# Blocks 2 and 3 of a fused recurrence and max-out kernel: second layer by seven products, the last product over three banks, and three chunks' transposes in halves

## The chip, the cores and the metric

The kernel runs on one core of a Trainium2 chip. The metric is the device time of one execution in microseconds (us), as the median of several runs. A core has five engines with instruction streams of their own: TensorE (PE in the profile, with its weight loads as PEld), VectorE (DVE), ScalarE (ACT), GpSimd (POOL) and SyncE (SP), which here only issues DMAs. An engine runs its stream in program order and waits on semaphores for the others.

## The reference

Two stages, one after the other. A gated recurrence runs over 6144 time steps, for 4 sequences of 256 features. Its 24576 x 256 output goes through a layer that takes the larger of two products and multiplies it with a third matrix.

```python
def _attn_ref(x, f_logit, lower_bound):          # x, f_logit: (4, 6144, 256)
    sig = 1.0 / (1.0 + np.exp(-f_logit))
    f = lower_bound[None, None, :] + (1.0 - lower_bound[None, None, :]) * sig
    i = 1.0 - f
    for t in range(S):
        h = f[:, t] * h + i[:, t] * x[:, t]
        y[:, t] = h
    return y

def _moe_ref(x, w1, w2, w_out):                  # (24576, 256), (256, 1024) twice, (1024, 256)
    h1 = x @ w1
    h2 = x @ w2
    g = np.maximum(h1, h2)
    return g @ w_out
```

## The kernel before

**Tiling.** Time is cut into 48 blocks of 512 steps, 12 to a sequence. Features lie on the 128 partitions in two halves, so a block's y is two tiles of 128 x 512. Blocks 0 to 3 come in chunks of their own; from chunk 4 on a chunk holds 1024 steps, that is a pair of blocks. Pair p is blocks 2p and 2p + 1, and belongs to chunk p + 2. Pairs from `PAIR0` = 2 on are worked on as pairs.

**Input.** GpSimd loads f_logit and x of a chunk with a cast to 16 bits into a scratch in DRAM (`fetch`, L96). `cross(c)` (L143) issues two transposing DMAs from SP, scratch to the tiles `fT` and `xT` (L148), then a tiny GpSimd copy of one element of fT (`pool_waits`, L341), behind which the loads of chunk c + 1 are issued. So each chunk's load follows the landing of the fT before it.

**Recurrence.** A gate is a sigmoid on ScalarE (`gate` L197 for blocks 1 to 3, `pair_gate` L273 for a quarter of a pair: one half of the features, one block). On VectorE follow two `decay` instructions (L207), one `drive` (L217) and two scans (L224) per block. The scan writes y into the same tile that later holds the block's hidden values.

**First layer** (`first_layer`, L428). max(h1, h2) is written as h1 + ReLU(h2 - h1), with the difference of the weights in `wd`. One slot is one of 8 groups of 128 hidden units: two matmuls of 128 x 512 into half of a `dT` tile. Two dT tiles of two banks each exist. Each second slot ends with a ReLU on ScalarE (L442), which empties a dT tile.

**Second layer.** It multiplies the 8 hidden groups by w_out, and the two halves of y by the product w1 w_out (`w13`): ten left factors of 128 rows, for each of 4 groups of 128 tokens. Done directly (`second_layer`, L462, blocks 0 to 3) that is 40 matmuls with 256 columns, called in eight pieces of five. A copy then leaves each of two banks, on ScalarE for blocks 0 and 3 and on VectorE for 1 and 2 (L489).

For the pairs it is done with seven products instead of eight of half the width (`sevenths`, L517): the two blocks, the two halves of the inner sum and the two halves `lo` and `hi` of the columns are a 2 x 2 by 2 x 2 product. VectorE makes four sums of hidden tiles (`sum1` to `sum4`, L499; sum3 first, sum2 from sum3, sum4 from sum2). The right factors' sums t1 to t4 are made once. Each product is 20 steps, a step being one matmul of 128 columns, so that a pair is 140 steps (`NSEV`), over three banks X, E and B:

- X takes block 2p's first inner half; `seed` then copies X into bank B with ScalarE (L543).
- E takes sum1 (steps 20 to 39); a `snapshot` to SBUF follows (L549).
- X goes on with sum2 (from step 40), a snapshot follows; B takes its second product and is copied out (L559); X takes sum3 and leaves with an add of a snapshot (L561).
- E takes sum4 and leaves with an add; X takes the last product (from step 120) and is copied out.

For the last pair of all (`end`) the last product is split: groups 0 and 1 go on in bank X, groups 2 and 3 each go into a fresh bank Y (one of the dT tiles) and get the snapshot of X added on leaving (L582). Each leaves with a store of its own, on the queues of SP and ScalarE.

**Order.** The order is written out by hand. Blocks 2 and 3 run their first layer with one piece of direct second layer of the block before behind each slot (L747 to L768). From pair 2 on, a loop over 16 slots per pair issues a slot of first layer, then steps of the sevens of the pair before, as many as `due` has grown by, then a `cross` at slot 2, then gates of the next pair at slots 4, 6, 12 and 14, then from `seq` what VectorE has to do, each entry with a key in units of ninths of a slot. During pair 2 the second layer of block 3 runs directly in seven of the slots, and its last piece in pair 3.

## Time and profile before

| | us |
|---|---|
| median of 7 runs | 378.54 |
| lowest, highest | 377.94, 380.01 |
| the profiled execution | 378.82 |
| its span, first to last instruction | 377.0 |
| TensorE at its clock | granted 1.000 of full speed |

Some groups from the page, by line, with their count and mean duration:

| line | what | count | mean ns |
|---|---|---|---|
| L434 | first layer, matmul of 512 columns | 768 | 379 |
| L480 | direct second layer, matmul of 256 columns | 160 | 273 |
| L643 | step of the sevens, matmul of 128 columns | 3080 | 219 |
| L442 | ReLU out of dT, ScalarE | 192 | 1023 |
| L499 | sum of hidden tiles, VectorE | 88 | about 1480 |
| L561 | leave with an add, VectorE | 44 | 683 |
| L549 | snapshot, ScalarE | 44 | 587 |
| L148 | transposing DMA, fT | 22 | 5.8 us to landing |
| L148 | transposing DMA, xT | 22 | 5.0 us to landing |

Matmuls are pipelined: the next begins before the one before has ended, so their durations add up to more than the time. What one costs is seen from start to start, in the chain that ended last. The same holds, less strongly, for VectorE and ScalarE.

Three stages can be told apart: the start to 11 us with weights and first blocks, a start-up with direct second layers to 56 us, and then 20 pairs alike. At the end, from 363 us on, only the last pair's sevens and its stores are left.

### The profile page before, as it was taken

To read this page: it belongs to the slowest core of one execution; us is meant where nothing else is said; L and a number is where in the kernel's file an instruction comes from. 1 tells how busy PE (TensorE), PEld (TensorE's weight loads), DVE (VectorE), ACT (ScalarE), POOL (GpSimd) and SP (SyncE) were. 2 spreads that over 40 slices of the span, in tenths; PEclk is the share of its full clock that TensorE was granted. 3 is DMA by queue.
4 is the path that set the end of the run, shared out by engine and by line. 5 is a ranking of instruction groups with operands and counts; after the bars stand their busy time and mean duration, and the time that the engine had idled before them with its cause. 6 is when DMAs were issued, how large, how long until landed. Compare 5 with 4: busy or idle time off the path is not lost.

```text
span 377.0 us, 9634 instructions
## 1 busy us (share of the span) xinstructions
PE 367.8 (98%) x4156; PEld 280.1 (74%) x4156; DVE 338.1 (90%) x408; ACT 303.2 (80%) x412; POOL 38.5 (10%) x80
## 2 busy tenths in 40 slices
PE   6899999999999999999999999999999999999995
PEld 5577767777777777777777777777777777777784
DVE  5796889999999999999999999999999999999762
ACT  4866798888888798788888888887988888888752
POOL 1401111110110100210101101101101101000000
PEclk9999999999999999999999999999999999999999
DMA  8999989999999979999989969999999989940223
GB/s 267 233 202 247 223 171 197 206 202 220 279 187 192 295 122 243 266 164 219 273 156 254 275 135 200 284 184 225 263 187 265 249 148 235 196 184 2 114 113 112
DMA packets 104543, 77.17 MB, mean 205 GB/s; under 512 B 93298, under 2 KB 95348, under 8 KB 103796
## 3 DMA queue, kind: packets, MB, share of 16 engines
q1 hardware_dynamic: 101536, 51.19, 60.2%
q0 software_dynamic: 2544, 25.17, 34.7%
q8 instruction: 32, 0.52, 0.6%
q10 hardware_dynamic: 420, 0.20, 0.2%
q14 instruction: 11, 0.09, 0.1%
HBM read 53.48 MB, written 48.23 MB: 270 GB/s over the span
## 4 chain that ended last, share of the span: by engine, by line
PE 95%; DMA 2%; ACT 1%; SPq 0%; DVE 0%; issue 0%; DVEq 0%
PE ps L643 45%; PE dT L434 44%; PE ps L480 5%; DMA r<-in_moe_w_dram 2%; PE ps L174 1%; PE ps L390 0%; SPq L117 0%; ACT r L345 0%; ACT S L349 0%; PE ps L376 0%; DVE osb L561 0%; DVE osb L582 0%; ACT sn L574 0%; PE dT L643 0%; DVEq L561 0%
## 5 line engine op out<-in xcount | busy, mean ns | idle before, releaser
L442 ACT ACTIVATE r<-dT 128x1024 f16<-128x1024 f32 x192 | 196.1, 1023 | 53.5 <-PE dT L434 53.3
L434 PE MATMUL dT<-r,wd 128*128 128x512 f16 x768 | 225.1, 379 | 0.0
L643 PEld LDWEIGHTS <-S 128*128 128x128 f16 x1760 | 115.5, 101 | 37.2 <-DVE S L499 0.2
L643 PEld LDWEIGHTS <-r 128*128 128x128 f16 x1320 | 90.9, 101 | 36.8 <-issue 0.2
L224 DVE TENSOR_TENSOR_SCAN r<-ff,r,v 128x512 f16<-128x512 f16 x88 | 108.1, 1269 | 0.8
L643 PE MATMUL ps<-t,S 128*128 128x128 f16 x1320 | 101.6, 219 | 0.0
L499 DVE TENSOR_TENSOR S<-r 128x2560 f16<-128x2560 f16 x44 | 65.4, 1486 | 15.3 <-ACT r L442 15.3
L434 PEld LDWEIGHTS <-wd 128*128 128x128 f16 x768 | 67.6, 113 | 4.7 <-DVE wd L358 0.4
L643 PE MATMUL ps<-wob,r 128*128 128x128 f16 x704 | 69.9, 219 | 0.0
L499 DVE TENSOR_TENSOR S<-r,S 128x2560 f16<-128x2560 f16 x44 | 64.9, 1475 | 0.0
L279 ACT ACTIVATE u<-fT 128x512 f16<-128x512 f16 x88 | 56.1, 638 | 0.0
L341 POOL CAST waited<-fT 128x1 f32<-128x1 f16 x22 | 12.7, 578 | 277.8 <-DMA fT<-scr 277.8
L207 DVE TENSOR_SCALAR ff<-u,nom 128x512 f16<-128x512 f16 (+1 forms) x98 | 31.6, 344 | 9.2 <-ACT u L201 3.2
L643 PE MATMUL ps<-w,r 128*128 128x128 f16 x176 | 38.5, 219 | 0.0
L643 PE MATMUL ps<-t,r 128*128 128x128 f16 x430 | 34.1, 219 | 0.1
L561 DVE TENSOR_TENSOR osb<-ps,sn 128x512 f32<-128x512 f32 x44 | 30.1, 683 | 3.2 <-PE ps L643 3.2
L643 PE MATMUL ps<-wob,S 128*128 128x128 f16 x352 | 32.6, 219 | 0.0
L217 DVE TENSOR_TENSOR v<-u,xT 128x1024 f16<-128x1024 f16 x44 | 30.0, 683 | 0.0
L549 ACT COPY sn<-ps 128x512 f32<-128x512 f32 x44 | 25.8, 587 | 2.0 <-PE ps L643 2.0
L559 ACT COPY osb<-ps 128x512 f32<-128x512 f32 x43 | 25.0, 582 | 0.8 <-PE ps L643 0.8
L480 PEld LDWEIGHTS <-r 128*128 128x128 f16 x160 | 16.0, 101 | 6.6
L643 PE MATMUL ps<-w,S 128*128 128x128 f16 x88 | 19.3, 219 | 0.0
(58 smaller groups left out, 132.6 us busy)
## 6 DMA issues: line engine op xcount, KB each, us to landing
out_dram<-osb SPq DMA_DIRECT2D x46, 512.0 KB, 3.9
scr<-in_f_logit_dram POOLq DMA_DIRECT2D x22, 512.0 KB, 7.2
scr<-in_x_dram POOLq DMA_DIRECT2D x22, 512.0 KB, 10.2
r<-in_moe_w_dram SPq DMA_DIRECT2D x4, 512.0 KB, 6.8
fT<-in_f_logit_dram POOLq DMA_DIRECT2D x3, 256.0 KB, 8.4
xT<-in_x_dram POOLq DMA_DIRECT2D x3, 256.0 KB, 9.0
out_dram<-osb SPq DMA_DIRECT2D x3, 256.0 KB, 2.5
osb<-in_f_logit_dram SPq DMA_DIRECT2D x2, 256.0 KB, 3.5
```

The lines of the kernel that those rows point to most:

```text
L207: nc.vector.tensor_scalar(out=ff[:, h, cols], in0=u[:, h, cols], scalar1=nom[:, h : h + 1], scalar2=1.0, op0=ALU.mult, op1=ALU.add,)
L217: nc.vector.tensor_tensor(out=like(v[:, :, cols], xT), in0=like(u[:, :, cols], xT), in1=xT, op=ALU.mult,)
L224: nc.vector.tensor_tensor_scan(out=y_of(j, h), data0=ff[:, h, o : o + TB], data1=v[:, h, o : o + TB], initial=0.0 if t0 == 0 else y_of(j - ...
L279: nc.scalar.activation(out=mids[p + NBLK, "u"][:, h, cols], in_=held[c, 0][:, h, cols], func=AF.Sigmoid, scale=-1.0,)
L434: nc.tensor.matmul(dT[:, fc % 2, :], lhsT=wd[:, kc, unit_cols(fc)], rhs=y_of(j, kc), start=(kc == 0), stop=(kc == KC - 1),)
L442: nc.scalar.activation(out=rts[j, k][:, g - 1 : g + 1, :].rearrange("p q (i m) -> p q i m", m=P), in_=dT[:].rearrange("p q (m i) -> p q i ...
L480: nc.tensor.matmul(ps[:, r, :], lhsT=left, rhs=right, start=(s == 0 and r == 0), stop=(s == n - 1 and r == 1), skip_group_check=True,)
L499: nc.vector.tensor_tensor(out=t[:], in0=a, in1=b, op=op)
L549: nc.scalar.copy(out=t[:], in_=bank[b][:])
L559: nc.scalar.copy(out=dst, in_=bank[b][:])
L561: nc.vector.tensor_tensor(out=dst, in0=bank[b][:], in1=snap[name][:], op=ALU.add)
L643: nc.tensor.matmul(bank[b][:, i, :], lhsT=a[:, k, cols], rhs=w, start=fresh, stop=after is not None, skip_group_check=True,)
```

## The change

Pair 1 (blocks 2 and 3) gets its second layer from `sevenths(1)`. Its steps run from slot 1 of pair 2 on, 8.75 a slot, and in pair 3 the rate is 15/16 of that. Block 1's direct second layer, which ran in eight pieces through block 2, now runs in pieces at every second slot of blocks 2 and 3, and its two copies are one on VectorE and one on ScalarE. Block 3's recurrence stands wholly in front of block 2's loop; the gates of pair 2 and the first half of its recurrence move into block 2's loop, the second half of decay and drive into pair 2. In pair 1 bank B is not seeded: X is kept as a snapshot, B opened fresh, and the snapshot added on leaving.

In the last product of all, group 0 goes first, into a fresh bank, then groups 1 and 2 in bank X, then group 3 in a fresh bank; groups 0 to 2 are stored together.

The transposing DMAs of the chunks below `FINE` = 7 are issued in two halves of 512 steps, and GpSimd waits for the second half of fT.

```diff
--- before.py
+++ after.py
@@ -36,8 +36,8 @@
     FC = DFF // P
     TB = 512
     CH = 1024
-    LAG = 2
     NSEV = 7 * 4 * 5
+    FINE = 7
     assert S % CH == 0
 
     chunks = []
@@ -145,9 +145,14 @@
 
         for s in range(2):
             dst = inpool.tile([P, KC, CH], HALF, name=("fT", "xT")[s])
-            nc.sync.dma_start_transpose(out=dst[:], in_=scratch[s][c % NSCR][:])
+            step = TB if c < FINE else CH
+            for o in range(0, CH, step):
+                nc.sync.dma_start_transpose(
+                    out=dst[:, :, o : o + step],
+                    in_=scratch[s][c % NSCR][o : o + step, :],
+                )
             held[c, s] = dst
-        pool_waits(held[c, 0][:, 0, 0:1])
+        pool_waits(held[c, 0][:, 0, CH - 1 : CH])
         if c + 1 < NCHUNK:
             for s in range(2):
                 fetch(c + 1, s)
@@ -486,7 +491,7 @@
                 skip_group_check=True,
             )
             if r == 1 and s == n - 1:
-                (nc.scalar.copy if j in (0, 3) else nc.vector.tensor_copy)(
+                (nc.vector.tensor_copy if j and g == 0 else nc.scalar.copy)(
                     out=osb[:, 2 * g : 2 * g + 2, :], in_=ps[:]
                 )
                 if i == ns - 1:
@@ -531,7 +536,7 @@
             steps[-1][-1] = fn
 
         def open_bank(b, i=0):
-            if i:
+            if b == "Y":
                 t = ps_d.tile([P, 2 * TB // P, P], FP32, name="dT")
             else:
                 t = ps_o.tile([P, TB // P, P], FP32, name="ps")
@@ -571,21 +576,23 @@
             def go():
                 leave(b, jb, hi, 5, False)()
                 t = snpool.tile([P, TB // P, P], FP32, name="sn")
-                nc.scalar.copy(out=t[:, 2:4, :], in_=bank[b][:, 2:4, :])
+                nc.scalar.copy(out=t[:, 0:4:3, :], in_=bank[b][:, 0:4:3, :])
                 snap[4] = t
             return go
 
         def leave_last(at):
             def go():
                 dst = osbs[jb][:, at, lo]
-                if at.start:
+                if at.start != 1:
                     nc.vector.tensor_tensor(
                         out=dst, in0=bank["Y"][:, at, :], in1=snap[4][:, at, :],
                         op=ALU.add,
                     )
                 else:
                     nc.scalar.copy(out=dst, in_=bank["X"][:, at, :])
-                store(jb, osbs[jb], at, lo, nc.sync if at.start == 2 else nc.scalar)
+                if at.start:
+                    part = slice(0, 3) if at.start == 1 else at
+                    store(jb, osbs[jb], part, lo, nc.scalar if at.start == 1 else nc.sync)
             return go
 
         def sub(n):
@@ -601,8 +608,11 @@
         def given(t):
             return lambda k: t[:, k, :]
 
+
+
+        begin = p == PAIR0 - 1
         product("X", part(0, 0), plain(0, lo), True)
-        then(seed("B", "X"))
+        then(snapshot("X", 1) if begin else seed("B", "X"))
         product("E", sub(1), given(t1), True)
         then(snapshot("E", 5))
         if end:
@@ -615,16 +625,15 @@
             then(leave_both("X"))
             product("E", sub(4), plain(1, hi))
             then(leave("E", ja, hi, 2, True))
-            product("X", part(1, 1), given(t4), groups=range(2))
-            then(leave_last(slice(0, 2)))
-            for i in (2, 3):
-                product("Y", part(1, 1), given(t4), True, groups=range(i, i + 1))
-                then(leave_last(slice(i, i + 1)))
+            for i, n in ((0, 1), (1, 2), (3, 1)):
+                b = "X" if n == 2 else "Y"
+                product(b, part(1, 1), given(t4), n == 1, groups=range(i, i + n))
+                then(leave_last(slice(i, i + n)))
         else:
             product("X", sub(2), given(t2))
             then(snapshot("X", 2))
-            product("B", part(0, 1), plain(1, lo))
-            then(leave("B", ja, lo, None, False))
+            product("B", part(0, 1), plain(1, lo), begin)
+            then(leave("B", ja, lo, 1 if begin else None, False))
             product("X", sub(3), given(t3))
             then(leave("X", jb, hi, 5, False))
             product("E", sub(4), plain(1, hi))
@@ -743,32 +752,27 @@
         turn(turn_steps(3))
         gate(3)
         cross(5)
-        early = scan_steps(3)
+        for step in scan_steps(3):
+            step()
+        scans = {PAIR0: pair_scans(PAIR0)}
         for fc in range(FC):
             first_layer(2, fc)
-            second_layer(1, fc)
-            if fc < 4:
-                early[fc]()
+            if fc > 3:
+                pair_gate(PAIR0, fc - 4)
+            if fc == 5:
+                for t in ("decay0", "drive0", "scan00", "scan01"):
+                    scans[PAIR0][t]()
+            if fc % 2:
+                second_layer(1, fc // 2)
         cross(6)
-        scans = {PAIR0: pair_scans(PAIR0)}
-        gates = {0: 0, 1: 1, 4: 2, 5: 3}
-        order = {
-            2: ("decay0", "drive0"),
-            3: ("scan00",),
-            4: ("scan01",),
-            6: ("decay1",),
-            7: ("drive1",),
-        }
         for fc in range(FC):
             first_layer(3, fc)
-            second_layer(2, fc)
-            if fc in gates:
-                pair_gate(PAIR0, gates[fc])
-            for t in order.get(fc, ()):
-                scans[PAIR0][t]()
+            if fc == 4:
+                sum3(1)
+            if fc % 2:
+                second_layer(1, 4 + fc // 2)
 
         queue, due = [], 0
-        pieces3, piece = (1, 3, 5, 9, 11, 13, 15), 0
         for p in range(PAIR0, NPAIR):
             first = p == PAIR0
             more = p + 1 < NPAIR
@@ -777,32 +781,31 @@
                 (36, scans[p]["scan11"]),
                 (112, lambda: sum3(p)),
             ]
+            if first:
+                seq += [(9, scans[p]["decay1"]), (10, scans[p]["drive1"])]
             if more:
                 scans[p + 1] = pair_scans(p + 1)
                 seq += [
-                    (64, scans[p + 1]["decay0"]),
-                    (66, scans[p + 1]["drive0"]),
-                    (70, scans[p + 1]["scan00"]),
-                    (84, scans[p + 1]["scan01"]),
+                    (73 if first else 64, scans[p + 1]["decay0"]),
+                    (75 if first else 66, scans[p + 1]["drive0"]),
+                    (79 if first else 70, scans[p + 1]["scan00"]),
+                    (93 if first else 84, scans[p + 1]["scan01"]),
                     (131, scans[p + 1]["decay1"]),
                     (133, scans[p + 1]["drive1"]),
                 ]
-            if not first:
-                seq += [
-                    (9, lambda: sum1(p - 1)),
-                    (18, lambda: sum2(p - 1)),
-                    (50, lambda: sum4(p - 1)),
-                ]
-                queue += sevenths(p - 1)
+            seq += [
+                (0 if first else 9, lambda: sum1(p - 1)),
+                (18, lambda: sum2(p - 1)),
+                (50, lambda: sum4(p - 1)),
+            ]
+            queue += sevenths(p - 1)
             seq.sort(key=lambda e: e[0])
-            gates = {4: 0, 6: 1, 12: 2, 14: 3} if more else {}
+            gates = {5 if first else 4: 0, 7 if first else 6: 1, 12: 2, 14: 3}
+            gates = gates if more else {}
             for slot in range(2 * FC):
                 first_layer(2 * p + slot // FC, slot % FC)
-                if first and slot in pieces3 or p == PAIR0 + 1 and slot == 1:
-                    second_layer(2 * PAIR0 - 1, piece)
-                    piece += 1
-                if p > PAIR0 + 1 or (p == PAIR0 + 1 and slot >= LAG):
-                    due += NSEV / (2 * FC)
+                if slot or not first:
+                    due += NSEV / (2 * FC) * (15 / 16 if p == PAIR0 + 1 else 1)
                     while due >= 1:
                         due -= 1
                         queue.pop(0)()
```

## The prediction

> **What bounds the kernel now.** I read the page's busy row first, then the chain that ended last.
>
> ```profile
> PE 367.8 (98%) x4156; PEld 280.1 (74%) x4156; DVE 338.1 (90%) x408; ACT 303.2 (80%) x412; POOL 38.5 (10%) x80
> PE 95%; DMA 2%; ACT 1%; SPq 0%; DVE 0%; issue 0%; DVEq 0%
> ```
>
> The first row alone proves little; the second says that the end is reached through TensorE work almost without a break from 11.1 us on. So the time falls by whatever matmul time goes, unless a wait takes its place. VectorE at 90% is the next candidate. The chain in order of time gives prices, first beside block 2, then over one pair (slot 0 of pair 4 to slot 0 of pair 5):
>
> ```profile
> 28.14 0.43 PE dT L434 x2
> 28.57 0.55 PE ps L480 x5
> 29.12 0.43 PE dT L434 x2
> ```
> ```profile
> 68.78 0.43 PE dT L434 x2
> 69.21 0.50 PE ps L643 x9
> ...
> 83.50 0.43 PE dT L434 x2
> ```
>
> A slot of first layer (two matmuls) plus five direct matmuls takes 29.12 - 28.14 = 0.98 us: 0.433 for the first layer, 0.545 for the five, 0.109 each. A pair takes 83.50 - 68.78 = 14.72 us: 16 x 0.433 = 6.92 and 140 steps of the sevens in 7.80, 0.0557 each.
>
> VectorE's order of time over that pair (start, duration, line, tile):
>
> ```profile
> 69.60 1.48 DVE L499 TENSOR_TENSOR S<-r 128x2560 f16<-128x2560 f16 x1
> 71.00 1.48 DVE L499 TENSOR_TENSOR S<-r,S 128x2560 f16<-128x2560 f16 x1
> 72.40 2.45 DVE L224 TENSOR_TENSOR_SCAN r<-ff,r,v 128x512 f16<-128x512 f16 x2
> 74.77 1.46 DVE L499 TENSOR_TENSOR S<-r,S 128x2560 f16<-128x2560 f16 x1
> 76.15 0.61 DVE L207 TENSOR_SCALAR ff<-u,nom 128x512 f16<-128x512 f16 x2
> 76.68 0.68 DVE L217 TENSOR_TENSOR v<-u,xT 128x1024 f16<-128x1024 f16 x1
> 77.39 2.46 DVE L224 TENSOR_TENSOR_SCAN r<-ff,r,v 128x512 f16<-128x512 f16 x2
> 80.41 1.49 DVE L499 TENSOR_TENSOR S<-r 128x2560 f16<-128x2560 f16 x1 [0.56 <-ACT r L442]
> 81.82 0.68 DVE L561 TENSOR_TENSOR osb<-ps,sn 128x512 f32<-128x512 f32 x1
> 82.42 0.79 DVE L207 TENSOR_SCALAR ff<-u,nom 128x512 f16<-128x512 f16 x2
> 83.12 0.69 DVE L217 TENSOR_TENSOR v<-u,xT 128x1024 f16<-128x1024 f16 x1
> 83.72 0.69 DVE L561 TENSOR_TENSOR osb<-ps,sn 128x512 f32<-128x512 f32 x1
> ```
>
> Durations overlap their neighbours, so I take start to start: a sum 1.40, two scans 2.37, a pair of decays 0.53 (0.70 after an add), a drive 0.65, an add 0.60. Its one wait in 14.72 us is 0.56: VectorE has 0.6 us of slack per pair.
>
> Two more rows, of ScalarE and of GpSimd:
>
> ```profile
> 51.23 1.06 ACT L442 ACTIVATE r<-dT 128x1024 f16<-128x1024 f32 x1
> 52.15 0.67 ACT L279 ACTIVATE u<-fT 128x512 f16<-128x512 f16 x1
> 52.67 1.06 ACT L442 ACTIVATE r<-dT 128x1024 f16<-128x1024 f32 x1
> ```
> ```profile
> 31.17 0.18 POOL L341 CAST waited<-fT 128x1 f32<-128x1 f16 x1 [15.15 <-DMA fT<-scr]
> ```
>
> Back to back, a ReLU holds ScalarE 0.92 us and a gate 0.52. Chunk 4's whole f had landed at 31.17.
>
> **What the Trainium skill says.** "Perfetto Trace Analysis", Identifying the Most-Contended Engine, calls matmul busy share a poor measure and asks for weight-load busy share; here that is only 74%, so I rest on the chain. "TensorE: Matmul & The Clock Gate", "Wait — 56ns, not 53.3ns?", gives N/2.4 GHz plus some 2.5 ns per warm matmul; the trace's 0.0557 at N = 128 and 0.109 at 256 agree. "PSUM — Partial Sum Buffer", PSUM bank collisions, wants two engines kept off one bank; at the end the trace has TensorE resuming at 371.27, just after ScalarE's copy out of the same bank (370.85 + 0.37).
>
> **The change, part by part.**
>
> *Sevens for blocks 2 and 3.* Removed: 80 direct matmuls, 80 x 0.109 = 8.72 us. Added: 140 steps, 7.80. Net -0.92 on TensorE. Block 1's second layer, moved to every other slot, costs the same.
>
> *Does ScalarE keep up while that layer is thinned?* A pair of slots now lasts 0.865 + 0.545 = 1.41 us. Counting from 28.14, block 3 starts at 33.79, its slot 2 at 35.20, pair 2 at 39.44. ScalarE after gate(3) (28.25): ReLUs at 29.17 and 30.45; gate 0 at 31.37; ReLU 31.89, gates 1 and 2, ReLU 33.85 to 34.87. The dT tile wanted at 35.20 is free 0.33 us early. Cost nothing; the cover is that 0.33 and f landing by 31.37. Block 3's scans end at 31.15 + 2.45 = 33.60, before its first layer needs the second at 34.0.
>
> *VectorE in pair 2.* Added for pair 1: four sums and three adds, of which only two direct copies go (j = 1 keeps one on VectorE, j = 2 loses two, j = 3 had none). After the scans of block 4 (end 37.3, wanted at 39.44), one copy and sum3, VectorE waits for block 3's last ReLU, so the run starts there. Block 3's last first-layer matmuls end at 38.89, the ReLU at 39.95. Then, in program order without a gap: sum1, decay1, drive1, sum2, two scans, sum4, decay0, drive0, scan, add, scan, add, sum3, add, decay1, drive1, sum1 of pair 2. That is five sums 7.0 and the last one's full end (0.08), four scans 4.77, three decay pairs 1.76, three drives 1.96, three adds 1.80: 17.4. With ReLU and hand-over (1.10) the sum is ready 18.5 us after 38.89.
>
> TensorE asks for it at step 20 of pair 2's product list, behind 9 left-over steps: 0.545 + (16 + 4) slots x 0.433 + (131 + 29) steps x 0.0557 = 18.1 us after 38.89, at 57.0. So it waits 0.4 us. Earlier demands (sum1 at 42.3 against 41.5, sum2 at 44.26 against 44.05, block 5's second scan at 46.5 against 46.4, bank X at 52.6 against 52.7) have little or no slack, but a short wait there comes out of the same 0.4, since VectorE's run does not depend on it. After it, block 7's scan (61.2 against 61.4) fits, and VectorE regains about 0.6 us per pair. I put 0.45 with the hand-over. Bounds: 0 if each VectorE instruction is 2% quicker; 0.9 if drives and decays take their slower forms (0.72 and 0.70).
>
> *Snapshot in place of seed, B fresh.* One ScalarE copy to SBUF (0.59) for one into PSUM (0.57), and a leave of VectorE's instead of ScalarE's, counted above.
>
> *Transposes in halves.* Four SP issues instead of two for three chunks, same bytes. One issue holds SP 1.8 to 3.1 us; halves should hold about half each. Behind them on SP stands only the store of block 1, which now also lies behind cross(6), to about 56; its buffer is not needed before pair 3's adds. POOL's wait is for the second half, which I take to land when the whole did. Deadlines: gate 0 at 31.37 (whole f at 31.17), pair 3's gates at 45.4 (37.48 + 5.4 = 42.9), pair 4's at 57.4 (50.72 + 4.6). Value 0. From below there is nothing to gain, as no gate waited long enough for TensorE to notice; from above 1 us if each half carries its own fixed part.
>
> *The last product.* Today TensorE idles 0.25 us (371.02 to 371.27) for the copy out of bank X, and two ACT issues follow one another to 373.40. Now group 0 goes into another bank meanwhile (5 steps, 0.28), so TensorE ends 0.25 earlier, and the last issue, on SP, ends near 373.2. But bytes flow at about 340 GB/s from 372.9 to 374.2, started by the 256 KB store issued at 371.90, which doesn't move. So I take -0.1, between -0.3 and +0.1.
>
> Sum against the profiled execution (378.82: span 377.0 and 1.8 around it): -0.92 + 0.45 - 0.1 = -0.57. From the median of 378.54 that gives **377.97 us**.
>
> **Rivals.** What this kernel's measurement can tell from no change is about 0.2%, 0.76 us.
> - *A, one short wait for sum1 of pair 2*: as above, 377.97, between 377.65 and 378.25. For it: the two sums 18.5 and 18.1. Chance 0.45.
> - *B, TensorE never waits*: -0.92 - 0.1, 377.5. For it: the wait is a difference of two long sums, 2% apart. Against: VectorE's durations repeat within 1%. Chance 0.27.
> - *C, VectorE at the slow end*: wait 0.9 or more, gain eaten, 378.5. Chance 0.09.
> - *D, slower: gate 0 blocks ScalarE.* Gate 0 moves from 36.38 to 31.37, in front of the ReLUs in ScalarE's in-order queue. If chunk 4's first half of f lands after 31.7, each microsecond more holds two ReLUs, then the dT tiles, then TensorE, one for one; from 33.0 it outweighs 0.57 + 0.76. With landing at 34 (two transposes sharing the rings and each paying its own latency) the time is 378.54 - 0.57 + 2.3 = 380.3. For it: landings of transposes spread from 4.4 to 9.7 us after issue. Against: this one landed 5.8 after issue as a whole, and a half has less to move. Chance 0.19, with lesser waits of this kind at chunks 5 and 6.
>
> **How the numbers follow.** Faster: B nearly whole (0.25) and a quarter of A (0.11), 0.36. Slower: D, with a little taken off for landings between 32.5 and 33.0 and a little of C put on, 0.19. Same: 0.45. The range runs from B with the larger tail gain, 377.2, to 379.4, a first step into D. The likeliest case's own range is 377.65 to 378.25.
>
> **What would show it.** In the changed profile: L643 with 3220 matmuls and L480 with 80; in the list of waits a new "PE ps L643 <- DVE S" of about 0.4 us near 57, none elsewhere over 0.2; ScalarE's gates of pair 2 from about 31.4, not released by a DMA; TensorE's last matmul 0.25 us nearer the end of the sums of the last pair. Wrong would be: no such wait (B), a wait over 0.8 (C), or ScalarE released by "DMA fT" with dT waits of TensorE near 34 to 37 (D).

## The result and the profile after

The changed kernel takes 384.97 us (median of 27 runs, 378.4 to 388.19) against 379.04 us of the kernel before (64 runs on the same chip): 1.0077 times, 95% interval 1.0058 to 1.0096. The ratio leaves out runs that are more than 1.5% above their kernel's fastest, 16 of the changed kernel's and none of before's, so it is less than the quotient of the medians (1.016). The forecast was 377.97 us, 377.2 to 379.4; the time lies outside, on the slower side.

The profiled execution took 385.71 us, its span 383.9, against 378.82 and 377.0 before. The page after, with the busy row, the chain's shares by engine, and the row of VectorE's leaves with an add (its last part is VectorE's idle time ahead of them):

```profile
PE 369.8 (96%) x4216; PEld 281.6 (73%) x4216; DVE 343.0 (89%) x412; ACT 304.6 (79%) x415; POOL 40.3 (10%) x80
PE 88%; DMA 7%; DVE 1%; ACT 1%; SPq 1%; issue 0%; ACTq 0%; DVEq 0%
L566 DVE TENSOR_TENSOR osb<-ps,sn 128x512 f32<-128x512 f32 x47 | 32.1, 683 | 8.4 <-DMA out_dram<-osb 5.2
```

DMA had 2% of the chain and now has 7%; TensorE fell from 95% to 88%. A transfer is on the path now. The list of waits of the changed kernel (total us, times, longest) says who stands still:

```profile
ACT u L284 <- DMA fT<-scr: 0.7, 1, 0.7
DVE osb L566 <- DMA out_dram<-osb: 5.2, 1, 5.2
PE ps L652 <- DVE osb L566: 5.9, 2, 5.1
```

TensorE waits 5.1 us in one piece for a leave of VectorE, which waits for a store: the leave writes a buffer that is still being read by block 1's store. The chain in order of time (start, us, what) leads there:

```profile
57.94 1.29 SPq L150
59.34 13.16 DMA out_dram<-osb
72.60 0.70 DVE osb L566
73.71 0.85 PE dT L439 x2
```

The store is issued behind the last half transpose, at 59.34, and takes 13.16 us to land. In the kernel before, the store of block 1 went out at 42.34 and landed after 3.7 us; behind chunk 6's transposes stood block 2's store, issued at 55.24, and it landed after 3.3. The last line has a second loss: two first-layer matmuls take 0.85 us, twice the 0.43 of before. Windows of the changed kernel show why (the column before the last two is TensorE's granted clock):

```profile
66.00:70.00 4.00, 2.23 (x28) 1.69 (x27) 1.40 (x2) 2.57 (x3) 0.00 (x0) 1.00 0.24 76
70.00:74.00 4.00, 0.66 (x4) 0.38 (x4) 1.40 (x4) 0.00 (x0) 0.00 (x0) 0.65 1.13 203
74.00:78.00 4.00, 4.00 (x25) 2.63 (x24) 4.00 (x5) 1.55 (x2) 2.32 (x3) 0.50 1.13 315
```

After the idle 5 us TensorE runs at half clock up to 78.2 us: some 4.9 us of work at half speed, a loss of 2.4. The Trainium skill says the same of long gaps ("TensorE: Matmul & The Clock Gate", What's actually happening: half clock after at least one idle window of about 3.4 us, full speed after at least one busy window of that length); the trace agrees, with 5.1 us of idle time ahead of the fall and 4.9 us of work up to the return.

The sum over the profiled execution: the two waits for leaves, 5.1 + 0.8, and the half clock, 2.4, less the 0.8 by which TensorE's stretch shrinks without the halves (e2, below) and the 0.7 by which block 2 happened to start earlier (27.26 against 27.98), make +6.8 of the +6.9 us. The sevens are there, and the waits have swallowed them. The question is what made the store late.

### The profile page after: what moved, and what is told of

Same layout as the page of the kernel before. It is cut to its first block, busy times and chain, and to the rows that moved or that the text cites. A ratio compares the mean times of both kernels' runs of the same rounds, so it can differ in the third digit from the quotient of the medians.

```text
span 383.9 us, 9767 instructions
## 1 busy us (share of the span) xinstructions
PE 369.8 (96%) x4216; PEld 281.6 (73%) x4216; DVE 343.0 (89%) x412; ACT 304.6 (79%) x415; POOL 40.3 (10%) x80
## 4 chain that ended last, share of the span: by engine, by line
PE 88%; DMA 7%; DVE 1%; ACT 1%; SPq 1%; issue 0%; ACTq 0%; DVEq 0%
PE ps L652 44%; PE dT L439 40%; DMA out_dram<-osb 3%; PE ps L485 2%; DMA fT<-scr 2%; DMA r<-in_moe_w_dram 1%; PE ps L179 1%; DVE r L229 1%; DVE osb L566 0%; SPq L150 0%; PE ps L395 0%; SPq L117 0%; ACT r L350 0%; ACT u L284 0%; ACT S L354 0%; PE ps L381 0%
## 5 line engine op out<-in xcount | busy, mean ns | idle before, releaser
L652 PEld LDWEIGHTS <-S 128*128 128x128 f16 x1840 | 120.9, 101 | 39.5 <-DVE S L504 0.2
L652 PEld LDWEIGHTS <-r 128*128 128x128 f16 x1380 | 96.0, 102 | 45.4 <-issue 8.0
L652 PE MATMUL ps<-t,S 128*128 128x128 f16 x1380 | 106.6, 219 | 0.0
L504 DVE TENSOR_TENSOR S<-r 128x2560 f16<-128x2560 f16 x46 | 68.3, 1485 | 16.0 <-ACT r L447 16.0
L652 PE MATMUL ps<-wob,r 128*128 128x128 f16 x736 | 73.0, 219 | 0.0
L504 DVE TENSOR_TENSOR S<-r,S 128x2560 f16<-128x2560 f16 x46 | 67.8, 1474 | 0.0
L346 POOL CAST waited<-fT 128x1 f32<-128x1 f16 x22 | 14.9, 675 | 283.0 <-DMA fT<-scr 283.0
L652 PE MATMUL ps<-t,r 128*128 128x128 f16 x450 | 37.0, 223 | 5.9 <-DVE osb L566 5.9
L566 DVE TENSOR_TENSOR osb<-ps,sn 128x512 f32<-128x512 f32 x47 | 32.1, 683 | 8.4 <-DMA out_dram<-osb 5.2
L548 ACT COPY ps<-ps 128x512 f32<-128x512 f32 x22 | 12.6, 571 | 3.2 <-PE ps L652 0.6
```

Of the source, the lines that this page charges most:

```text
L346: nc.gpsimd.tensor_copy(out=waited[:], in_=t)
L504: nc.vector.tensor_tensor(out=t[:], in0=a, in1=b, op=op)
L566: nc.vector.tensor_tensor(out=dst, in0=bank[b][:], in1=snap[name][:], op=ALU.add)
L652: nc.tensor.matmul(bank[b][:, i, :], lhsT=a[:, k, cols], rhs=w, start=fresh, stop=after is not None, skip_group_check=True,)
```

## Experiments

All were compared with the kernel before on the same chip, in five groups (medians of before 378.76, 379.03, 378.43, 379.04 and 379.05). In the table, "SP holds" is how long SP was busy with issuing fT's transposes of chunks 4, 5 and 6; "margin" is the start of GpSimd's next load of f less the end of SP's issue of xT's transposes (negative: the load goes out while SP is still at it); "next" is from that load to the issue of the next chunk's fT. Late rounds stand under "next"; the four largest all go with margins of -0.6 or less, but g1 (-0.8) and g2 (-0.5) show no late round.

| kernel | SP holds, us | margin, us | next, us | ratio (95%) |
|---|---|---|---|---|
| before | 2.4, 2.6, 1.8 | 0.8, 1.3, 1.5 | 5.9, 7.2, 5.2 | 1 |
| changed | 4.1, 4.5, 4.6 | 0.0, 0.9, -0.6 | 6.9, 5.0, 9.1 | 1.0077 |
| e1, store first | 3.6, 4.7, 6.5 | 0.2, -0.2, 0.5 | 8.1, 6.5, 5.8 | 1.0068 (1.0037 to 1.01) |
| e2, whole transposes | 2.4, 2.6, 2.7 | 0.9, 1.8, 0.8 | 5.9, 5.0, 6.3 | 0.998 (0.9968 to 0.9992) |
| e3, fifth buffer | 4.4, 3.4, 4.4 | -0.8, 0.4, 1.7 | 13.2, 6.3, 5.8 | 1.0062 (1.0033 to 1.0092) |
| e4, before with halves | 4.5, 3.9, 3.6 | -0.8, 0.5, 0.3 | 16.1, 8.1, 5.7 | 1.0033 (1.0008 to 1.0057) |
| e5, e2 with the store first | 2.4, 1.9, 2.9 | 1.0, 1.0, 1.0 | 6.4, 7.8, 5.3 | 0.9991 (0.9979 to 1.0003) |
| g1, halves by features | 4.5, 5.2, 5.0 | -0.8, 1.3, 1.1 | 6.4, 5.3, 7.6 | 1.0249 (1.0191 to 1.0308) |
| g2, only fT in halves | 4.5, 4.6, 3.8 | -0.5, 2.3, 3.5 | 7.0, 5.1, 5.2 | 1.0095 (1.0056 to 1.0134) |
| g3, unbroken targets | 4.1, 4.5, 3.6 | 0.1, 1.1, 0.4 | 6.2, 5.0, 7.4 | 1.005 (0.9997 to 1.0103) |
| g4, loads behind xT | 4.5, 3.6, 4.8 | 3.2, 2.5, 3.0 | 5.0, 5.0, 5.3 | 1.0219 (1.0191 to 1.0248) |
| h2, g4 and the store first | 4.1, 3.6, 4.3 | 3.6, 3.6, 2.9 | 5.1, 5.1, 5.2 | 1.025 (1.0221 to 1.0279) |
| i1, only chunk 4 in halves | 4.5, 4.7, 2.8 | -0.8, 1.2, 1.5 | 13.3, 5.1, 6.0 | 1.0073 (1.0024 to 1.0122) |
| i3, only xT in halves | 2.4, 2.8, 2.7 | 0.7, 0.7, 2.9 | 6.3, 6.3, 5.5 | 1.0004 (0.9982 to 1.0027) |
| i4, whole, SP held | 2.4, 3.6, 2.7 | 0.0, 0.0, 1.3 | 8.0, 7.2, 5.8 | 1.0117 (1.0083 to 1.0152) |
| i5, halves, loads later | 4.2, 3.6, 4.5 | 1.5, 2.1, 0.9 | 6.0, 5.0, 6.2 | 1.0159 (1.0126 to 1.0193) |

### e1: the store goes first

The nearest suspect is the store's place behind chunk 6's transposes. `cross(6)` moves behind block 3's loop.

```diff
-        cross(6)
         for fc in range(FC):
             first_layer(3, fc)
...
+        cross(6)
```

> The changed kernel with cross(6) moved from ahead of block 3's loop to behind it, so that SP issues the store of block 1 before it waits for chunk 6; halves kept. Theory 1 (the store's place on SP): the store is issued near 46 instead of 59.3, block 5's osb buffer is free long before 67, the 5.1 us wait of TensorE and the half clock after it go, and the time falls to 377.5 to 378.8. Theory 2 (the halves, which hold SP 4.0 to 4.6 us where a whole transpose held it 1.8 to 3.3 and so make the whole chain of chunks late): little helps that leaves the halves in; the gates of pair 3 still wait near 45 and the time stays above 380. In both the 0.8 us wait in pair 2 stays.

385.18 us. The store was issued at 47.93, long before the 59.34 of the changed kernel, and the time did not fall. It stood just behind a load of GpSimd's (47.60), as the changed kernel's did (58.62), and took 10.8 us to land. The waits changed place: VectorE 3.2 us for a store, ScalarE 3.2 us in three pieces for fT at its gates. The store's place behind chunk 6's transposes alone does not explain the loss.

### e2: whole transposes

```diff
-    FINE = 7
+    FINE = 4
```

> The changed kernel with whole transposes (FINE = 4), the store of block 1 still behind cross(6). Theory 1: the store is issued about 55 to 57, still a risk; if its lateness alone decides, it lands late in some runs and the time stays spread, 379 to 386. Theory 2: the chain of chunks is back to that of before (51 and 55 on SP), the gates of pair 3 don't wait, the store lands within 4 us, and the time is 377.5 to 378.5 with a small spread.

378.17 us, 0.2% faster than before. Its page:

```profile
PE 367.9 (98%) x4216; PEld 279.9 (74%) x4216; DVE 343.0 (91%) x412; ACT 304.5 (81%) x415; POOL 39.7 (11%) x80
PE 94%; DMA 4%; SPq 0%; POOL 0%; issue 0%; DVE 0%
```

The sevens and the new last product stay in it, and no engine but GpSimd waits for a transposing DMA, and none for a store. So all of the loss comes with the halves. The store is issued at 55.03 here, again behind `cross(6)`. The trace does not show when it landed, but no engine waits for it: its place is harmless when the transposes are whole.

### e3: a fifth output buffer

```diff
-    opool = ctx.enter_context(tc.tile_pool(name="opool", bufs=4))
+    opool = ctx.enter_context(tc.tile_pool(name="opool", bufs=5))
```

> The changed kernel with five osb buffers instead of four, nothing else. Block 5 then takes a buffer that nothing holds, so the store of block 1 may land when it likes. If the wait for that buffer is what costs the time, 377.5 to 378.8 with no wait of VectorE for a store, though the store itself is as late as in the changed kernel. If the late chain of chunks costs time by itself, over 380.

385.01 us, no gain. The 5.2 us wait for the store's buffer went, and others took its place: 6.5 us of VectorE for xT, 4.0 of ScalarE for fT. The wait that the changed kernel shows is one of several heirs of the same lateness.

### e4: the kernel before with the halves alone

```diff
-            nc.sync.dma_start_transpose(out=dst[:], in_=scratch[s][c % NSCR][:])
+            step = TB if c < FINE else CH
+            for o in range(0, CH, step):
...
```

> The kernel before with the halves alone (chunks 4 to 6, and GpSimd waiting for the second half). Theory 1: no store is moved, so no wait appears: 378.4 to 379.2, the same as before. Theory 2: the chain of chunks is about 1 us later; block 2's store, issued behind cross(6), comes later too, and the time rises by 0.5 us or more.

384.45 us (1.015 times by the medians, 1.0033 by the ratio). The halves do it alone, without the sevens. GpSimd's order of time shows the loads of chunk 5 and the wait for its fT, 22 us later; windows show that the DMA engines stood nearly still for a part of that time (the last two columns are their share, over 1 where transfers overlap, and GB/s):

```profile
32.14 0.49 POOL L101 DMA_DIRECT2D scr<-in_f_logit_dram  x1 [0.26 <-issue]
32.62 0.49 POOL L101 DMA_DIRECT2D scr<-in_x_dram  x1
54.88 0.18 POOL L347 CAST waited<-fT 128x1 f32<-128x1 f16 x1 [21.77 <-DMA fT<-scr]
```

```profile
36.00:40.00 4.00, 4.00 (x31) 2.98 (x29) 1.04 (x2) 2.70 (x4) 0.00 (x0) 1.00 2.08 146
40.00:44.00 4.00, 4.00 (x31) 3.00 (x29) 3.58 (x5) 3.23 (x5) 0.00 (x0) 1.00 0.15 7
```

The loads of 32.14 and 32.62 landed after 16.1 and 18.9 us, xT's second half after 16.8, the store after 19.4; in the start-up of the kernel before, loads took 5 to 9 us and stores 3 to 4. With 7 GB/s moving from 40 to 44 us this is not a lack of bandwidth: something waits for something that the trace does not show.

### g1 to g3: what the halves look like

Is it the shape? g1 halves by features, so that each target is one unbroken tile and all 1024 steps are in it. g3 halves by time, into tiles laid out so that each half's target is unbroken. g2 halves only fT.

```diff
# g1
-                    out=dst[:, :, o : o + step],
-                    in_=scratch[s][c % NSCR][o : o + step, :],
+                    out=dst[:, k : k + step, :],
+                    in_=scratch[s][c % NSCR][:, k * P : (k + step) * P],
# g2
-            step = TB if c < FINE else CH
+            step = TB if c < FINE and s == 0 else CH
# g3
+                dst = inpool.tile([P, 2, KC, TB], HALF, name=("fT", "xT")[s])
...
+                        out=dst[:, t, :, :],
```

> The changed kernel with each of the twelve split transposes cut by features instead of by time: 1024 rows of 128 features, so that a half fills one unbroken run of 2 KB in each partition; as many DMAs as in the changed kernel. Theory 2a (four transposes under way at once, whatever their shape, stall the queue): the late landings stay and so does the time, 380 to 388 with a wide spread. Theory 2b (a half's shape does it: 512 rows, a run of 1 KB in a row of 2 KB): the stalls go, 377.5 to 378.5 with a spread under 3.

> The changed kernel with only fT in halves and xT whole: three transposes under way in place of four. Theory 2a: between the two, with fewer late landings, a median of 379 to 382. Theory 2b: halves of either kind stall, 380 to 386. If only xT's halves matter (in one trace a second half of xT took 16.8 us to land, fT's never over 6.9), 377.5 to 378.5.

> The changed kernel with the halves by time as before, but each half into a part of the tile that is unbroken in every partition (2 x 512 elements), the readers changed to match. Theory 2a: no help, 380 to 388. Theory 2b in its form that the broken destination matters: 377.5 to 378.5; in its form that the 512 rows matter: no help.

391.8, 383.37 and 383.24 us. No shape's median is free of the loss; g3's runs reach from 378.6 to 387.61, so its interval touches no change, but its median is 1.1% above before. g1's chain leads over xT's second half of chunk 4, which took 10.8 us to land. g2 is the telling one: with fT alone in halves, a whole transpose of xT lands late too (8.9 us for chunk 4), and VectorE waits 4.5 us for xT.

### g4 and h2: GpSimd's loads behind xT

Next suspect: GpSimd's loads start while xT is still under way. In g4 GpSimd also waits for xT's second half before it loads; h2 adds the edit of e1.

```diff
         pool_waits(held[c, 0][:, 0, CH - 1 : CH])
+        if c < FINE:
+            pool_waits(held[c, 1][:, 0, CH - 1 : CH])
```

> The changed kernel with GpSimd also waiting for xT's second half, for the split chunks, before it issues the next chunk's loads, so that no load is under way beside the split transposes. Theory 2c (the halves stall because the loads, on the other queue, come between them): the late landings of transposes go, though the chain of chunks gets 2 to 3 us longer per chunk; transposes land in 4 to 6 us, and the time is 378 to 381. Theories 2a and 2b: the transposes still land late, above 8 us in some, and the time is 382 or more.

> The changed kernel, halves kept, with both: GpSimd waits for xT's second half too before the next loads, and cross(6) stands behind the store of block 1. With the loads held back alone the transposes landed in 3.2 to 4.8 us and the runs stayed within 1 us of each other, at 387.7, with VectorE waiting 5.4 us for the store of block 1. If loads beside transposes make the landings late and the store's place makes the late chain dear, this has neither: the 5.4 us wait goes, 2 to 3 us of gates waiting for fT stay, 379 to 382 with a spread under 2. If the store's place is of no account, 386 or more.

The landings came out as theory 2c had them, the times did not. In g4 the transposing DMAs of chunks 4 to 6 (one landing is not in the trace) land in 3.2 to 5.1 us, the stores among them in 3.1 to 3.7, the loads in 4.9 to 8.3: the lateness is gone, so it came from loads beside what SP issues, not from the halves as such. But the time is 387.66 us, longer than the changed kernel's. The added wait is 6.4 us in three pieces, about 2 us a chunk, and it lies in a ring: transposes, GpSimd's wait, loads, next transposes. h2 moves the store out of the way, and its time is 387.72: 5.7 us above the 382 of the theory, and in the range of its rival, 386 or more. Its chain has the ring on it:

```profile
55.37 4.32 DMA fT<-scr
59.77 0.63 ACT u L286
60.40 0.92 ACT r L449
70.47 5.59 DMA fT<-scr
76.08 0.63 ACT u L286
```

The gates of chunks 6 and 7 wait for fT, since fT's issues come at 24.72, 40.19, 55.37 and 70.47: 15.1 to 15.5 us apart. In e2 they come at 25.84, 38.38, 49.92 and 61.99, 12.1 apart on average. Chunk 7 arrives 8.5 us later, which is more than the start-up can spare.

### e5, h3, h4: the parts without halves

e5 is e2 with the edit of e1; h3 is the kernel before with the new last product alone; h4 is e2 with the old last product.

```diff
# h4
-            for i, n in ((0, 1), (1, 2), (3, 1)):
...
+            product("X", part(1, 1), given(t4), groups=range(2))
+            then(leave_last(slice(0, 2)))
+            for i in (2, 3):
...
```

> The changed kernel with whole transposes and cross(6) behind the store of block 1. With whole transposes alone the time was 0.998 of the kernel before. The store's place matters only where it lands late: the same ratio, 0.997 to 0.999, 377.8 to 378.4.

> The kernel before with the new last product alone (group 0 in a fresh bank, then 1 and 2, then 3; two stores). By the prediction -0.1 us, between -0.3 and +0.1: a ratio of 0.9992 to 1.0003; TensorE's wait of 0.25 us ahead of the last product goes. If the last issue sets the end, -0.2 to -0.3; if the bytes of the 256 KB store do, 0.

> The changed kernel with whole transposes and the old last product: the sevens for blocks 2 and 3 alone. By the prediction -0.92 + 0.45 = -0.47 us, a ratio of 0.9988; with no wait at all -0.92, 0.9976. TensorE's short waits in pairs 2 and 3 should add up to 0.3 to 0.5 us.

378.16 us; 378.04 us, 0.9991 times (0.9973 to 1.0008); 379.23 us, 1.0014 times (1.0 to 1.0029). By the time, the parts do not add up: e5 and h3 lie between e2 and before, h4 on the slow side of before. In the trace h4 has the sevens' gain: from the start of block 2's first matmul to the start of the last of all it takes 343.81 us, against 344.35 before (e2 takes 343.54). That h4's median does not show it is not explained; block 2's start alone moved between 27.1 and 29.8 us over the profiled executions.

### i1 to i3: how many chunks, which ones, which tensor

Two ideas were left for the mechanism: a slip of the ring that adds up over three chunks, or a single collision.

```diff
# i1: only chunk 4
-    FINE = 7
+    FINE = 5
# i2: only chunks 7 and up
-            step = TB if c < FINE else CH
+            step = TB if c >= FINE else CH
# i3: only xT, chunks 4 to 6
+            step = TB if c < FINE and s == 1 else CH
```

> Only chunk 4's transposes are in halves; chunks 5 and 6 are whole. Theory 'slip adds up' (each split chunk lengthens the round transposes - GpSimd's wait - loads - next transposes by about 2 us, against some 2 us of slack at the gates): one slip fits, no wait of TensorE over 0.5 us, next fT issues about 39, 51, 63; 378 to 380. Rival 'one collision is enough' (the loads of chunk 5 land beside the split xT of chunk 4 late by themselves, as once in a run of the halves alone, where the next fT issue came 22.5 us after): median 382 to 385, and the spread as wide as that of the changed kernel.

> Chunks 4 to 6 whole, all 19 later chunks in halves. Theory 'no slack in the start-up': from chunk 7 on a round is paced by TensorE at 14 to 15 us and needs about 12 with whole transposes, 13.6 to 15.7 with halves, so the halves are mostly hidden: 378 to 381. Rival 'a split transpose costs by itself wherever it stands': 6 us for 3 chunks, so 30 to 40 us for 19: 400 or more.

> Only xT of chunks 4 to 6 in halves, fT whole. Theory 'fT's second half is late, so GpSimd's loads are' : without split fT the wait ends as with whole transposes (5 to 6 us after issue), 378 to 379. Rival 'the loads beside split xT transposes land late': loads land in 9 to 16 us, fT issues of chunks 5 and 6 later than 39 and 52, 382 to 386.

384.36, 396.59 and 379.38 us. i1: one chunk in halves costs as much as three (1.0073 against 1.0077), so a sum of slips falls; chunk 5's loads took up to 15.3 us and xT's second half of chunk 4 16.1. i2: halves in the 19 later chunks cost 17.5 us (1.0478 times, 1.0442 to 1.0513), 0.9 each; neither the 378 to 381 of a hidden cost nor the 400 of the rival. Its waits are VectorE's and ScalarE's for stores, and its chain leads over five stores that took 9.7 to 12.4 us:

```profile
DVE osb L566 <- DMA out_dram<-osb: 18.9, 9, 4.7
ACT osb L564 <- DMA out_dram<-osb: 10.1, 4, 4.2
```

i3 is the surprise: xT in halves costs nothing. Its SP queue for chunk 4 beside that of the changed kernel, each with GpSimd's load behind it (start, us held, what, how many):

```profile
25.89 2.39 SPq L150 DMA_TRANSPOSE fT<-scr  x1
28.38 3.37 SPq L150 DMA_TRANSPOSE xT<-scr  x2
```
```profile
32.43 0.49 POOL L100 DMA_DIRECT2D scr<-in_f_logit_dram  x1 [0.26 <-issue]
```

and of the changed kernel, chunks 4 and 6:

```profile
24.90 4.05 SPq L150 DMA_TRANSPOSE fT<-scr  x2
29.05 2.59 SPq L150 DMA_TRANSPOSE xT<-scr  x2
...
51.98 4.56 SPq L150 DMA_TRANSPOSE fT<-scr  x2
56.65 2.59 SPq L150 DMA_TRANSPOSE xT<-scr  x2
59.34 0.52 SPq L458 DMA_DIRECT2D out_dram<-osb  x1
```
```profile
31.65 0.49 POOL L100 DMA_DIRECT2D scr<-in_f_logit_dram  x1
...
58.62 0.49 POOL L100 DMA_DIRECT2D scr<-in_f_logit_dram  x1
```

Two halves of xT hold SP about as long as one whole (2.6 to 3.4 us here, 2.0 to 3.3 in e2), but two halves of fT hold it 4.1 to 4.6 us instead of 2.4 to 2.7: the first half takes about as long as a whole, and the second comes on top. Counted from fT's issue, xT's issue ends 1.2 to 2.9 us later in the changed kernel than before, and the store's comes behind it, while GpSimd's loads, released by fT's landing, go out only 0.4 us (chunk 4) and 0.7 us (chunk 6) later. In i3 the load comes 0.7 us after the end of xT's issue; in the changed kernel at the same moment (chunk 4) or 0.6 us before it (chunk 6). In chunk 4's round one store takes 11.1 us, for which nothing waits; chunk 6's is the round that goes wrong.

### i4 and i5: the hold made without halves, and met with halves

i4 has whole transposes, and between fT's and xT's SP issues four small reads that nothing uses. i5 is the changed kernel with a fill of a spare tile on GpSimd ahead of the loads.

```diff
# i4
+            if s == 0 and c < 7:
+                for q in range(4):
+                    pad = padpool.tile([P, 8], FP32, name="pad")
+                    nc.sync.dma_start(out=pad[:], in_=f_logit[0, 0:P, 8 * q : 8 * q + 8])
# i5
+        if c < FINE:
+            pad = padpool.tile([P, 1536], FP32, name="pad")
+            nc.gpsimd.memset(pad[:], 0.0)
```

> Whole transposes; between fT's and xT's of chunks 4 to 6 SP issues four added reads of 4 KB, some 0.5 us each, so xT's issue ends about 2 us later and GpSimd's loads fall on it, as they do with fT in halves. Theory 'loads fall on xT's issue': late landings (a transfer over 8 us among them), waits of 2 to 6 us at a gate, a drive or a leave, 381 to 386. Rival 'the two halves themselves' : 378 to 379 as with whole transposes.

> The changed kernel with a fill of a spare tile on GpSimd (about 1.4 us) between its wait for fT and the next loads of chunks 4 to 6. Theory 'loads fall on xT's issue': the loads now come 1 us or more behind the end of xT's issue, all transposes land within 6 us, and the round is 1.5 us longer than with whole transposes instead of 2 to 10: 378 to 381. Rival 'the two halves themselves' : the same late landings and 383 to 387.

i4: 390.21 us (its runs 383.43 to 393.86), above the 381 to 386 of the theory. The loss is there with not one transpose in halves; that the four added reads do harm of their own, besides holding SP, is not excluded. The profiled execution was one of its quicker ones (383.89); its SP queue and GpSimd's loads for chunk 5:

```profile
39.67 3.56 SPq L151 DMA_TRANSPOSE fT<-scr  x1
43.28 2.78 SPq L159 DMA_DIRECT2D pad<-in_f_logit_dram  x4
46.17 1.70 SPq L151 DMA_TRANSPOSE xT<-scr  x1
```
```profile
47.82 0.49 POOL L101 DMA_DIRECT2D scr<-in_f_logit_dram  x1
48.30 0.49 POOL L101 DMA_DIRECT2D scr<-in_x_dram  x1
```

The load goes out as xT's issue ends, at 47.87; the loads took up to 10.3 us to land and a store 11.5, and VectorE waited 4.5 us for xT.

i5: with the loads 0.9 to 2.1 us behind the end of xT's issue the transposing DMAs of chunks 4 to 6 (one landing is not in the trace) land in 3.3 to 5.3 us and the stores among them within 4.0, as the theory had it. The time, 384.51 us, is not what it had (378 to 381); it is in the range of the rival. What is left is the ring: its rounds take 14.3, 14.4 and 14.3 us instead of 12.1. Its waits, and the one DMA on its chain between 40 and 110 us, a store issued 0.3 us behind a load of a later round, where no fill stands:

```profile
PE ps L656 <- DVE osb L570: 4.4, 4, 2.1
DVE osb L570 <- DMA out_dram<-osb: 3.9, 2, 2.9
```
```profile
87.53 11.67 DMA out_dram<-osb
```

So there seem to be two prices, and one can be paid in place of the other: the loads either fall on xT's issue and the transfers land late, or they wait for it and the ring gets longer.

All 19 profiles together say more about both. Of the stores between 20 and 340 us whose landing the traces show, all 72 that SP issued 0.1 to 1.0 us behind the start of a load of f took 10.1 to 19.4 us to land; of 457 issued 0.3 to 3.0 us ahead of one, 430 took 6.0 at most. Each of the 72 landed 0.2 to 2.7 us after the load of x that goes out with that of f. The kernel before has such a store itself, at 68.11, 0.2 us behind the load: 12.2 us, and nothing waits for it. So a store is late where it falls behind a load, with whole transposes too; whether that costs time depends on when its buffer is due.

The ring's length sorts the kernels. From chunk 4's issue of fT to chunk 7's it takes 36.2 to 41.6 us in the seven profiles without the loss (before, e2, e5, g3, h3, h4, i3: 348.0 to 349.1 us from block 2's start to the end), and 42.5 to 50.1 in the eleven with it (353.4 to 358.9 us); i2, whose halves come later, stands apart. This sorts single executions; it is not a test of its own. The changed kernel has 42.8 against 36.7 before. Of these 6.1 us, 3.9 come from fT, which lands whole later, and 2.6 from the way from the load to the next fT, less 0.4 at GpSimd in between.

**The version to keep** is e2: sevens and new last product, transposes whole. 378.17 us, 0.998 times before, and quicker than the changed kernel by 1.8% of the medians, 1.0% by the ratios.

## Why the prediction was wrong

**The step that failed** is "Transposes in halves", with "Value 0". Two assumptions under it did not hold. The first is "halves should hold about half each". For xT they did (1.2 to 1.7 us each), for fT not: in the changed kernel its first half held SP 2.3 to 3.2 us, as long as a whole one in the start-ups without halves (1.8 to 3.3), and the two in a row 4.1 to 4.6. The second is "POOL's wait is for the second half, which I take to land when the whole did": counted from fT's issue it landed after 6.2, 7.6 and 5.9 us, the whole before after 5.8, 5.4 and 4.6. The bound from above, 1 us "if each half carries its own fixed part", named the fixed part, but priced only the halves' own lateness. In its place the runs show that the ring of chunks comes late, and that what SP issues comes level with GpSimd's loads or behind them and then lands late. This costs about 6 us by the medians (6.8 from e2 to the changed kernel, 5.7 from before to e4) and 1.0% and 0.3% by the ratios. A single chunk is enough (i1), and so, it seems, is holding SP without any halves (i4).

**"Behind them on SP stands only the store of block 1 ... its buffer is not needed before pair 3's adds"** was true of the place, and left out how long the store takes to land: 13.2 us in place of 3.7. A landing was taken as a constant of its DMA, where it goes with what else is issued at that moment: the store went out 0.7 us behind GpSimd's load of 58.62.

**Rival D**, slower, had the sign and the sort of cause, a late landing, but not the place. It had chunk 4's first half of f late at gate 0 of pair 2, with lesser waits at chunks 5 and 6; in the profiled execution no gate waited over 0.7 us, and where gates did wait longer, 4.9 us in e4 and 5.4 in i1, it was for chunk 5. What came late first were xT of chunk 4, the loads behind it and the store. Its 380.3 us was also too low.

**The sevens** were right in the trace. TensorE's stretch from block 2's first matmul to its last shrank by 0.54 us in h4, which has them alone (343.81 against 344.35); the terms were -0.92 and +0.45, so -0.47. h4's median does not show the gain.

**VectorE in pair 2** was right in size: in e2 the first sum of pair 2 was ready 18.3 us after block 3's last first-layer matmuls (39.80 to 58.06), predicted 18.5. The wait that follows is in e2's chain in order of time as two groups of nine steps that last 0.65 us in place of 0.50:

```profile
53.21 0.65 PE ps L652 x9
...
57.87 0.65 PE ps L652 x9
```

With 0.08 at 47.2 that makes 0.38, near the 0.45 taken, though in three places, not one; the list of waits shows none, as each is short.

**ScalarE keeps up** held: in e2 no gate waits for fT, and TensorE waits for no ReLU.

**The last product** was to make TensorE end 0.25 us earlier, and it does. From the first start to the last, the last 120 steps take 6.67 us in all 16 profiles that have it, and 6.94 to 6.95 in the three that do not (before, e4, h4). The pause for the copy out of bank X is gone; TensorE around it, before and in e2:

```profile
370.93 0.22 PE L643 MATMUL ps<-w,S 128*128 128x128 f16 x1
371.27 0.72 PE L643 MATMUL ps<-t,r 128*128 128x128 f16 x10
```
```profile
371.32 0.22 PE L652 MATMUL ps<-w,S 128*128 128x128 f16 x1
371.38 0.44 PE L652 MATMUL dT<-t,r 128*128 128x128 f16 x5
```

How much of it reaches the end is not shown: the stretch from the last step's start to the end of the span varies from 4.3 to 4.7 us with the old product and from 4.3 to 5.2 with the new. The term was -0.1; h3's ratio, 0.9991 (0.9973 to 1.0008), is compatible with it and with nothing at all.

Without the halves the sum fits what e2 measured: 377.97 against 378.54 is 0.9985, e2 has 0.998 (0.9968 to 0.9992). That is not a proof of the parts, since h4's 1.0014 and h3's 0.9991 do not add up to it.

## What to carry to other kernels

A DMA that is split can hold its queue longer than one whole, so ask what stands behind it on that queue and what is released in the meantime elsewhere: here one to three microseconds more on SP put one engine's loads on another's transposes and stores. Where a buffer is due soon, look at whether its store goes out ahead of another queue's load or just behind it. The Trainium skill says that splitting may let a task complete sooner where DMA engines are generally idle ("Perfetto Trace Analysis", DMA Optimizations). That was not the case here: on the page of the kernel before, their busy share is 8 or 9 tenths in every slice up to 140 us, and splitting fT alone cost about 1% (g2). Before a start-up stage is touched, write down its ring (here transposes, wait, loads, transposes) with its period and the slack at each reader, and price any edit in it by the period.

## What the runs showed of the hardware

- In the start-up (chunks 4 to 6 of all runs), a chunk's first transposing DMA, of fT, held SP's queue 1.6 to 3.8 us as a half (512 rows, in g1 1024 rows of half the features) and 1.8 to 4.7 as a whole (1024 rows); a second half of fT took another 1.3 to 2.9. A half of xT, which follows, took 1.2 to 2.2, a whole 1.7 to 4.2.
- When GpSimd's loads go out before SP has finished issuing xT's transposes, landings can become late: up to 16.8 us for xT, 18.9 for a load and 19.4 for a store, in place of 4 to 5, 5 to 9 and 3 to 4 in the start-up before, with the DMA engines' share at 0.15 between 40 and 44 us (all in e4). For the transposes and the loads it is a risk, not a rule: of four rounds of the table with a margin of -0.8, three took 13.2 to 16.1 us to the next fT and one 6.4. No round with a margin over 0.6 us took more than 7.8.
- For stores the order decided in all the traces: all 72 issued 0.1 to 1.0 us behind the start of a load of f took at least 10.1 us to land, each landing 0.2 to 2.7 us after the load of x; 430 of 457 issued 0.3 to 3.0 us ahead of a load of f took 6.0 at most. Why they hold each other up was not settled. "DMA: Bandwidth & Descriptors", Queues, rings and completion order, in the Trainium skill, has each DMA engine take turns between the queues by packets; that would lengthen all of them together, but does not explain engines at rest.
- One wait of 5.1 us cost TensorE another 2.4, by half clock for 4.9 us after it.
